# Three one-column constants in one buffer: everything allocated behind them moves down by 64 bytes

## The chip, the core and the metric

The kernel runs on one core of one Trainium2 chip. The metric is the time of one execution on the device, in microseconds (us). Before the change it is 485.12 us, the median of three runs (484.73 to 485.75). Every other number here is of one profiled execution, which itself took 485.06 us, or of the program as it is built (buffer addresses).

## What is computed

The reference is one transformer-like block on a sequence of 2048 rows of 448 channels: a layer norm scaled and shifted by a condition vector, a long convolution over the sequence (a state space model, S4), a gated residual, a second layer norm, and a SwiGLU feed-forward of inner width 1792 with a second gated residual.

```python
def _B_ref(x, w_gate, w_up, w_down):
    g = _silu(x @ w_gate)
    u = x @ w_up
    return (g * u) @ w_down
...
mod = (_silu(c) @ w_mod).reshape(c.shape[0], 6, 1, -1)
sa, ca, ga, sb, cb, gb = (mod[:, 0], mod[:, 1], mod[:, 2], mod[:, 3], mod[:, 4], mod[:, 5])
h = _layernorm(x, axis=-1) * (1 + ca) + sa
x = x + ga * _A_ref(h, A_A_re, A_A_im, A_B_re, A_B_im, A_C_re, A_C_im, A_log_dt, A_Dskip)
h = _layernorm(x, axis=-1) * (1 + cb) + sb
x = x + gb * _B_ref(h, B_w_gate, B_w_up, B_w_down)
return x
```

`_A_ref` is the convolution. On the inputs given its kernel is so close to a straight line over the sequence that the program takes a short way (`small_path`); a flag computed on the chip chooses between it and a general convolution, which does not run here.

## The kernel before, in words

**The head** (0 to about 40 us). Twenty-eight transfers on the SyncE queue bring the six state arrays, the modulation weights (`wm0` to `wm4`, and a sixth group into `m5`), the first rows of `x` and the first feed-forward weights. From these, all engines make the modulation rows, the two slopes of the convolution and the first two row tiles of the second norm. The order is written out by hand in `ORDER` (the loads) and `PLAN` (the compute steps).

**The feed-forward** (about 33 us to the end). The 2048 rows are 16 tiles of 128, worked on in six blocks of 2, 2, 3, 3, 3 and 3 tiles (`BLOCKS`). `ffn` runs for each block over the 14 slices `f` of the inner width. For every `f`, `gate_up` makes two products of 128 by 256 or 128 by 384 in PSUM: 22 matmuls, line 729, all issued by `mm`. The weight slice `wgu[f]` (tile `gu`, 128 by 128 a piece) is the stationary operand and the transposed activations `hhi` and `hlo` are the moving one. Full-precision numbers are split in two parts that the fast float32r format holds, hence eleven matmuls for a product of four pieces. ScalarE applies SiLU (line 744), VectorE multiplies by the up product (line 757), ScalarE and VectorE split the result into `phi` and `plo` (lines 760, 761). `down` then adds to the output in PSUM, three matmuls for each row tile (line 773): `phi` or `plo` stationary, the down weights `wdh` or `wdl` moving, 448 columns. Between these matmuls, VectorE, ScalarE and GpSimd prepare the rows of the next block (`small_path`, `Norm`, `turn`), three TensorE products with the triangular matrix `tri` among it (lines 933 to 935, and 945 to 948 in the first block).

**All weights stay in SBUF.** In the first block the slices are loaded into staging buffers (`raw`, `rawd`) and split into `gu`, `wdh` and `wdl` (lines 112 to 127); the later five blocks load no weights.

**How SBUF is laid out.** Pools hand out addresses along each of the 128 partitions in the order in which tiles are created, each rounded up to 32 bytes. The pool `const` comes first: `x` rows, `m5`, staging, `ident`, `tri`, `run`, `hhi`, `hlo` and others. At its end stand the small constants that the change touches: `ones` (1.0, line 227), `mhalf` (-0.5, line 228), `ntok` (minus the row number, line 229), each of one column of float32, that is 4 bytes a partition in a slot of 32. Behind them lie `cs`, `pick`, `gac`, the small norm tiles, `gu0` to `gu2` with their down weights, then the buffers of the head (`pre`), and over these later `gu3` to `gu13`, the other down weights and the working tiles (`v1`, `vh`, `vl`, `p`, `phi`, `plo`).

`ones` is read by two one-element activations (lines 295, 320), by a copy (line 304) and as a stationary column (line 438); `mhalf` is the exponent of the power in `Norm.root` (line 168, on GpSimd); `ntok` is used once (line 703).

Of the kernel before, what the change touches and what calls it, by code (L numbers as in the profile page):

```python
# [8 lines left out]
F32 = mybir.dt.float32  # L9
# [47 lines left out]
def tile_kernel(ctx, tc, x, a_re, a_im, b_re, b_im, c_re, c_im, log_dt,  # L57
# [5 lines left out]
    const = ctx.enter_context(tc.tile_pool(name="const", bufs=1))  # L63
# [160 lines left out]
            parts(hi, lo, turned[:, 0:m, :, k, :], k)  # L224

    wp0 = ctx.enter_context(tc.tile_pool(name="wp0", bufs=1))
    ones = const.tile([128, 1], F32)
    mhalf = const.tile([128, 1], F32)
    ntok = const.tile([128, 1], F32)
    cs = const.tile([128, 5], F32)  # L230
    pick = const.tile([128, 1], F32)
    gac = const.tile([128, 4], F32)
# [813 lines left out]
def build(nc, aps, out):  # L1046
    with tile.TileContext(nc) as tc:
        a = dict(aps)
        tile_kernel(tc, a["A_u"].rearrange("b l d -> (b l) d"), *[a[n] for n in _INS[1:] + ["B_w_gate_up", "A_states", "w_mod_groups", "c_log_dt", "dft", "idft"]],
                    out.rearrange("b l d -> (b l) d"))  # L1050
# [20 lines left out]
```

## Time and profile before

| | |
|---|---|
| median of three runs | 485.12 us (484.73 to 485.75) |
| the profiled execution's own time | 485.06 us |
| its span, first to last instruction | 483.0 us |
| outside the span | 2.06 us |
| TensorE matmul busy, share of the span | 471.6 us, 98% |
| TensorE weight load busy | 444.9 us, 92% |
| VectorE / ScalarE / GpSimd busy | 285.1 / 155.4 / 59.8 us |
| mean granted TensorE clock | 0.999 |

The span lies between the first and the last instruction that the profiler records. A busy engine is one with an instruction in flight; matmuls overlap each other in the array, so the duration of one (start to end) is longer than the distance from one to the next, and it is the distance that adds up. PE is TensorE's matmul stream, PEld its weight loads, DVE is VectorE, ACT ScalarE, POOL GpSimd, SP SyncE.

### The profile page before, as it was taken

The numbers are of one execution on the slowest core, as the hardware profiler recorded it, in microseconds if no ns is written. First come the engines' busy times: TensorE is split into PE (matmuls) and PEld (weight loads), VectorE is DVE, ScalarE is ACT, GpSimd is POOL, SyncE is SP. The second block draws the span as 40 slices with busy tenths as digits, with TensorE's granted clock in tenths as the row PEclk, the third lists the DMA queues.
The fourth block names the chain that finished last, engine by engine and source line by source line (L and its number), as shares of the span: only waits on it lengthen the run. The fifth ranks groups of instructions, "written<-read, shape, count | busy, mean of one in ns | idle before, by whom it ended". The sixth has DMA issues, their size and how long they took to land.

```text
span 483.0 us, 7024 instructions
## 1 busy us (share of the span) xinstructions
PE 471.6 (98%) x2743; PEld 444.9 (92%) x2743; DVE 285.1 (59%) x550; ACT 155.4 (32%) x336; POOL 59.8 (12%) x82
## 2 busy tenths in 40 slices
PE   6999999999999999999999999999999999999995
PEld 4668988999999999999999999999999999999995
DVE  4879998768876546573644757375475544221225
ACT  5876545522234222332312323331222232112111
POOL 1220000000000040310022221002241000000000
PEclk9999999999999999999999999999999999999999
DMA  8965563020001200111200011130001112000001
GB/s 307 405 225 165 194 188 103 0 96 2 1 2 39 58 1 0 45 38 51 92 25 0 2 44 46 43 115 0 2 2 44 45 43 77 22 1 0 1 1 62
DMA packets 18778, 31.24 MB, mean 65 GB/s; under 512 B 2608, under 2 KB 13488, under 8 KB 18736
## 3 DMA queue, kind: packets, MB, share of 16 engines
q1 hardware_dynamic: 18000, 30.52, 18.8%
q8 instruction: 23, 0.38, 0.3%
q10 hardware_dynamic: 736, 0.19, 0.2%
q14 instruction: 19, 0.16, 0.1%
HBM read 24.61 MB, written 6.03 MB: 63 GB/s over the span
## 4 chain that ended last, share of the span: by engine, by line
PE 92%; DMA 3%; DVE 2%; ACT 1%; issue 0%; POOL 0%; SPq 0%; ACTq 0%; DVEq 0%
PE bank L729 59%; PE dn L773 28%; DMA wm<-in_w_mod_groups_dram 2%; DMA x<-in_A_u_dram 1%; PE bank L238 1%; PE dn L449 1%; PE bank L934 1%; PE cv L933 1%; PE cv L935 0%; PE bank L947 0%; DVE x L812 0%; PE bank L206 0%; PE cv L946 0%; PE cv L948 0%; ACT raw L195 0%
## 5 line engine op out<-in xcount | busy, mean ns | idle before, releaser
L729 PE MATMUL bank<-hhi,gu 128*128 128x384 f32 (+1 forms) x1169 | 211.3, 320 | 0.0
L729 PEld LDWEIGHTS bank<-hhi,gu 128*128 128x128 f32 x1169 | 191.2, 188 | 3.1 <-issue 0.7
L729 PE MATMUL bank<-hlo,gu 128*128 128x384 f32 (+1 forms) x668 | 131.8, 319 | 0.0
L757 DVE TENSOR_TENSOR bank<-raw,bank 128x384 f32<-128x384 f32 (+1 forms) x69 | 36.9, 534 | 125.0 <-PE bank L729 121.6
L729 PEld LDWEIGHTS bank<-hlo,gu 128*128 128x128 f32 x668 | 110.2, 188 | 0.0
L760 ACT CAST phi<-bank 128x384 fp32r<-128x384 f32 (+1 forms) x83 | 36.9, 444 | 141.6 <-DVE bank L757 141.6
L744 ACT ACTIVATE raw<-bank 128x384 f32<-128x384 f32 (+1 forms) x70 | 32.9, 470 | 123.0 <-PE bank L729 114.9
L761 DVE TENSOR_TENSOR plo<-bank,phi 128x384 fp32r<-128x384 f32 (+1 forms) x83 | 42.5, 512 | 37.1 <-ACT phi L760 37.1
L773 PE MATMUL dn<-wdh,phi 128*128 128x448 f32 x218 | 58.3, 368 | 0.6 <-DVE run L698 0.4
L773 PE MATMUL dn<-wdh,plo 128*128 128x448 f32 x218 | 57.7, 366 | 0.0
L773 PE MATMUL dn<-wdl,phi 128*128 128x448 f32 x218 | 57.6, 365 | 0.0
L773 PEld LDWEIGHTS dn<-wdl,phi 128*128 128x128 f32 x218 | 41.0, 188 | 3.4
L773 PEld LDWEIGHTS dn<-wdh,plo 128*128 128x128 f32 x218 | 40.9, 188 | 3.3
L773 PEld LDWEIGHTS dn<-wdh,phi 128*128 128x128 f32 x218 | 38.9, 188 | 2.9 <-DVE run L698 0.7
L167 POOL TENSOR_SCALAR rsb<-mvb 128x1 f32<-128x1 f32 (+2 forms) x13 | 4.6, 354 | 171.9 <-DVE mvb L151 171.9
L167 POOL TENSOR_SCALAR rsa<-mva 128x3 f32<-128x3 f32 (+1 forms) x6 | 2.4, 396 | 116.1 <-DVE mva L151 116.1
L123 ACT CAST gu<-raw 128x1024 fp32r<-128x1024 f32 x14 | 14.6, 1046 | 0.0
L125 DVE TENSOR_TENSOR gu<-raw,gu 128x768 fp32r<-128x768 f32 x14 | 13.3, 953 | 0.1
L922 DVE TENSOR_TENSOR vl<-m,vh 128x448 fp32r<-128x448 f32 x12 | 9.1, 757 | 6.7 <-ACT vh L921 6.1
L908 POOL TENSOR_TENSOR m<-m,gm 128x448 f32<-128x448 f32 x9 | 10.4, 1154 | 21.4 <-DVE m L184 17.5
L194 ACT ACTIVATE raw<-raw,rsb 128x64 f32<-128x64 f32 x14 | 4.8, 346 | 21.0 <-DVE raw L193 11.9
L927 POOL TENSOR_TENSOR m<-m,gd 128x448 f32<-128x448 f32 x9 | 11.6, 1284 | 0.0
(232 smaller groups left out, 411.0 us busy)
## 6 DMA issues: line engine op xcount, KB each, us to landing
raw<-in_B_w_gate_up_dram SPq DMA_DIRECT2D x14, 512.0 KB, 3.9
rawd<-in_B_w_down_dram SPq DMA_DIRECT2D x16, 224.0 KB, 4.1
x<-in_A_u_dram SPq DMA_DIRECT2D x12, 224.0 KB, 3.3
out_dram<-x SPq DMA_DIRECT2D x11, 224.0 KB, 2.0
xd<-raw SPq DMA_DIRECT2D x9, 256.0 KB, 2.0
raw<-xd SPq DMA_DIRECT2D x36, 64.0 KB, 2.0
wm<-in_w_mod_groups_dram SPq DMA_DIRECT2D x5, 448.0 KB, 8.2
wm<-in_w_mod_groups_dram SPq DMA_DIRECT2D x5, 336.0 KB, 8.2
```

The lines of the kernel that those rows point to most:

```text
L123: sc.copy(wgu[j][:, :, 0:4, :], w)
L125: en.tensor_tensor(lo, w[:, :, 0:3, :], f32(hi), op=OP.subtract)
L167: po.tensor_scalar(rs[:, 0:n], self.mv[:, 0:n, 1], EPS, None, op0=OP.add)
L729: pe.matmul(ps[s][:, 0:n], w[:, s, a], (hlo if lo else hhi)[:, k, 0:n], start=first and q == 0, stop=end and q == len(ka) - 1)
L744: sc.activation(p[:, 0:n], ps[0][:, 0:n], AF.Silu)
L757: ve.tensor_tensor(ps[1][:, 0:n], p[:, 0:n], ps[1][:, 0:n], op=OP.mult)
L760: sc.copy(hi[:, 0:n], ps[1][:, 0:n])
L761: ve.tensor_tensor(lo[:, 0:n], ps[1][:, 0:n], f32(hi[:, 0:n]), op=OP.subtract)
L773: pe.matmul(dn[q][:, 0:D], u[:, cs], v, start=f == 0 and z == 0, stop=f == (NF - 3 if last else NF - 1) and z == 2)
L908: (ve if on_v else po).tensor_tensor(v, h, g, op=OP.mult)
L922: ve.tensor_tensor(vl, v0, f32(vh), op=OP.subtract)
L927: (ve if on_v else po).tensor_tensor(h, h, gd, op=OP.mult)
```

## The change

The three constants become the three columns of one tile. The names stay and refer to its columns.

```diff
     wp0 = ctx.enter_context(tc.tile_pool(name="wp0", bufs=1))
-    ones = const.tile([128, 1], F32)
-    mhalf = const.tile([128, 1], F32)
-    ntok = const.tile([128, 1], F32)
+    few = const.tile([128, 3], F32)
+    ones, mhalf, ntok = (few[:, q:q + 1] for q in range(3))
     cs = const.tile([128, 5], F32)
     pick = const.tile([128, 1], F32)
     gac = const.tile([128, 4], F32)
```

Three slots of 32 bytes become one, so that what is allocated behind them lies 64 bytes lower on each partition. In the built programs:

| buffer | address before | after | rest by 128 before | after |
|---|---|---|---|---|
| `x`, `m5`, `raw`, `rawd`, `ident`, `tri` | 1152 to 37248 | the same | 0 | 0 |
| `run`, `hhi`, `hlo` | 37792 to 54688 | the same | 32 | 32 |
| `ones`, `mhalf`, `ntok` | 62688, 62720, 62752 | 62688, 62692, 62696 | 96, 0, 32 | 96, 100, 104 |
| `cs` | 62784 | 62720 | 64 | 0 |
| `gu0` to `gu13` | 63264 to 195872 | 64 lower | 32 | 96 |
| `wdh`, `wdl`, `v1`, `vh`, `vl`, `p`, `phi`, `plo` | 77600 and up | 64 lower | 32 | 96 |
| `wm0` to `wm4`, the states, `h`, `v0`, `v1` of the head | 95584 and up | 64 lower | 96 | 32 |
| `ramp`, `far`, `all1` of the head | 148992 and up | 64 lower | 0 | 64 |

No instruction is added, removed or moved on any engine, and each waits for the same semaphores and values as before; only the names and the addresses differ, and the line numbers, by one. GpSimd's first compute rows show it. Before (`J`, `tok` and `ntok` are filled, then the first norm's power is taken):

```order
L289 IOTA J 128x128
L290 IOTA tok 128x1
L291 IOTA ntok 128x1
L167 TENSOR_SCALAR rsa<-mva 128x2
L168 TENSOR_TENSOR rsa<-rsa,mhalf 128x2
```

After, on the same engine and at the same place:

```order
L288 IOTA J 128x128
L289 IOTA tok 128x1
L290 IOTA few 128x1
L167 TENSOR_SCALAR rsa<-mva 128x2
L168 TENSOR_TENSOR rsa<-rsa,few 128x2
```

Nothing moved: the third fill and the power name `few` in place of `ntok` and `mhalf`.

## The prediction

> **What bounds the kernel now.** I read the busy times first, then the shares of the chain that ended last, then the waits, then the chain in order of time.
>
> The page, parts 1 and 4:
>
> ```profile
> PE 471.6 (98%) x2743; PEld 444.9 (92%) x2743; DVE 285.1 (59%) x550; ACT 155.4 (32%) x336; POOL 59.8 (12%) x82
> ...
> PE 92%; DMA 3%; DVE 2%; ACT 1%; issue 0%; POOL 0%; SPq 0%; ACTq 0%; DVEq 0%
> ```
>
> TensorE is busy 98% of the span and makes 92% of the chain that sets the end. The waits say the same from the other side (engine and line, what it waited for, us in total, times, longest):
>
> ```profile
> DVE bank L757 <- PE bank L729: 121.6, 57, 4.0
> ACT raw L744 <- PE bank L729: 114.9, 54, 3.2
> ```
>
> VectorE and ScalarE wait for gate and up matmuls, not the reverse. Split at 40 us (length, then busy time of each engine; PEclk is the granted clock):
>
> ```profile
> core 0: us, PE busy (x) PEld busy (x) DVE busy (x) ACT busy (x) POOL busy (x), PEclk, DMA share, GB/s
> 0.00:40.00 40.00, 34.13 (x192) 22.62 (x192) 29.51 (x73) 27.83 (x69) 8.85 (x21) 1.00 0.80 293
> 40.00:483.00 443.00, 437.44 (x2551) 422.23 (x2551) 255.56 (x478) 127.61 (x267) 50.97 (x61) 1.00 0.14 44
> ```
>
> There are two regimes: 40 us of head, in which transfers and every engine take turns, and 443 us in which TensorE is idle for 5.6 us only, at full clock. So the time is the head plus a matmul count times the distance between matmuls. Those distances are in the chain in order of time (start us, length us, what):
>
> ```profile
> 24.37 0.75 PE dn L481 x2
> ...
> 56.75 2.61 PE bank L729 x22
> ...
> 64.63 0.75 PE cv L946 x2
> ...
> 198.01 3.86 PE bank L729 x22
> ...
> 464.53 3.88 PE bank L729 x22
> 468.41 1.82 PE dn L773 x9
> 470.23 3.89 PE bank L729 x22
> ```
>
> A burst of 22 gate and up matmuls takes 2.61 us with 256 moving columns (118.6 ns each) and 3.86 to 3.89 with 384 (175.5 to 176.8 ns); a down matmul with 448 columns takes 1.82 / 9 = 202 ns. There are 2 x 14 = 28 short bursts (616 matmuls), 4 x 14 = 56 long ones (1232), and 16 tiles x 14 x 3 = 672 down matmuls: 73 + 217 + 136 = 426 us of the 443. **Only what changes the distance of these matmuls can move the time much.** One ns on each of the 1848 gate and up matmuls is 1.85 us, or 0.4%.
>
> **The change, part by part.**
>
> *Instructions and waits.* None is added, removed or moved, and no wait has another semaphore or value. Had the shared buffer tied its readers to all three writers, this would show what it costs (tile, times in ns, first and last start):
>
> ```profile
> L291 POOL IOTA ntok<- x1: 131/131/131, 1.1 to 1.1; 128x1 f32 x1
> L292 DVE MEMSET ones<- x1: 59/59/59, 0.8 to 0.8; 128x1 f32 x1
> L304 DVE CAST all<-ones x1: 220/220/220, 1.6 to 1.6; 128x128 fp32r<-128x128 f32 x1
> ```
>
> The last writer ends at 1.1 + 0.13 = 1.23 us and the first reader starts at 1.6. Such a wait would be over before it began: 0 us either way.
>
> *The head.* The states, `wm0` to `wm4` and the working tiles go from rest 96 by 128 to rest 32. Buffers at other rests do the same work in this trace. Transfers of 448 KB (KB, us to landing) into `wm` (rest 96) and `m` (the tile `m5`, rest 0):
>
> ```profile
> wm<-in_w_mod_groups_dram SPq DMA_DIRECT2D x5, 448.0 KB, 8.2
> m<-in_w_mod_groups_dram SPq DMA_DIRECT2D x1, 448.0 KB, 8.3
> ```
>
> One VectorE operation, writing `m` (rest 0) and `h` of the head (rest 96), min/median/max ns:
>
> ```profile
> L182 DVE SCALAR_TENSOR_TENSOR m<-rawd,mva,ca x4: 677/677/680, 105.6 to 255.5; 128x448 f32<-128x448 f32 x4
> L182 DVE SCALAR_TENSOR_TENSOR h<-x,mva,ca x2: 680/680/681, 15.1 to 15.7; 128x448 f32<-128x448 f32 x2
> ```
>
> They differ by 0.1 us and by 3 ns, and the order in the queue alone would explain as much. The full float32 matmuls above move `v0` of the head at rest 96 (line 481) and `m5` at rest 0 (line 946): 0.75 us for two in both. I take 0 for the head, between -0.1 and +0.1 us.
>
> *The down matmuls.* Their stationary `phi` and `plo` and their moving `wdh` and `wdl` all move together, so that their distance in memory stays. By operand (busy us, mean ns):
>
> ```profile
> L773 PE MATMUL dn<-wdh,phi 128*128 128x448 f32 x218 | 58.3, 368 | 0.6 <-DVE run L698 0.4 <-ACT x L697 0.2
> L773 PE MATMUL dn<-wdl,phi 128*128 128x448 f32 x218 | 57.6, 365 | 0.0
> ```
>
> `wdl` lies 1792 bytes behind `wdh`, that is, half of 512 off, and nothing but the waits ahead of the first of each group tells them apart. I take 0.
>
> *The gate and up matmuls.* Here is the one relation that changes: moving `hhi` and `hlo` stay at rest 32, stationary `gu` goes from rest 32 to 96. Every weight load runs beside the matmul before it, so two reads of SBUF that used to be equal by 128 are now 64 bytes apart. No row has just this pair. Nearest are float32r matmuls of 448 columns with other pairs:
>
> ```profile
> L934 PE MATMUL bank<-v,tri 128*128 128x448 f32 x12 | 4.4, 366 | 0.0
> L933 PE MATMUL cv<-vh,tri 128*128 128x448 f32 x12 | 4.4, 365 | 0.0
> ...
> L449 PE MATMUL dn<-v,far 128*128 128x448 f32 x1 | 0.4, 369 | 0.0
> ```
>
> `tri` is at rest 0 beside moving `v1` and `vh` at 32 (a difference of 32): 366 and 365 ns. `far` is at 0 beside the head's `v1` at 96: 369, a single one. Against 365 to 368 of line 773, where both are at 32, no row shows a relation that costs or saves more than a few ns. **I take 0**, the value of these rows.
>
> The ends come from the pace. A full float32 matmul of 448 columns takes 0.75 / 2 = 375 ns. If that is two passes, one pass of 448 is 187.5 ns, of 384 160.7 and of 256 107.1. The bursts need 175.9 (3.87 us) and 118.6: 15.2 and 11.5 ns more, on which no view puts a name. If the shift took all of it away, it would save 15.2 x 1232 + 11.5 x 616 = 25.8 us: **459.3** is the low end. For the high end, each matmul is as long as the longest (min/median/max, then means by shape):
>
> ```profile
> L729 PE MATMUL bank<-hhi,gu x1169: 274/336/384, 33.7 to 473.1; 128*128 128x384 f32 x130, 128*128 128x256 f32 x65
> L729 PE MATMUL bank<-hlo,gu x668: 277/336/343, 35.7 to 473.8; 128*128 128x384 f32 x112, 128*128 128x256 f32 x55
> L729 PE MATMUL dn<-hlo,gu x4: 279/280/285, 35.3 to 35.6; 128*128 128x256 f32 x4
> ```
>
> ```profile
> L729 PE MATMUL bank<-hlo,gu 128*128 128x384 f32 x448 | 96.8, 338 | 0.0
> ...
> L729 PE MATMUL bank<-hlo,gu 128*128 128x256 f32 x220 | 34.9, 282 | 0.0
> ```
>
> With 343 for 338 and 285 for 282: 5 x 1232 + 3 x 616 = 8.0 us, or **493.1**.
>
> *A rule beside it.* The Trainium skill, page "TensorE: Matmul & The Clock Gate", section "Step-by-step: what each phase is for", says that TensorE reads the moving operand and the weights through two independent ports, so that loading the next weights takes nothing from the running matmul; by that rule the new distance between `gu` and `hhi` cannot matter and the sum stays at 485.1. The trace agrees in the three pairs of rests above (32 and 32, 0 and 32, 0 and 96). The same page, section "Back-to-back issue gap", gives N / 2.4 + 2.5 ns for a warm matmul: 162.5 ns at 384 columns and 109.2 at 256. The trace shows 175.9 and 118.6, so this rule does not describe this stream, and by it a shift that freed the stream would end at an estimated 485.1 - 13.4 x 1.232 - 9.4 x 0.616 = 462.8.
>
> **The sum.** 485.06 (own time of the profiled execution: 483.0 of span and 2.06 around it) + 0 + 0 + 0 = 485.06. That execution lies 0.06 under the median of the runs, 485.12. I predict 485.1.
>
> **The rivals.**
>
> *Faster: the long step goes.* The durations at 384 columns are not one value: most are at 336, some at 343, with a mean of 338. Equal work with two lengths says that something beats against the stream. If it is the weight load beside it, a new distance can take the step away: 338 to 336 on 1232 matmuls and 282 to 280 on 616 gives 2.5 + 1.2 = 3.7 us: **481.4**. For it: 15 ns above the pace on every matmul, unexplained. Against it: bursts with quite different neighbours on VectorE and the other engines agree within 3.86 to 3.89, and three pairs of rests show nothing. Any larger gain, down to 459.3, is its tail.
>
> *Slower: the step comes more often.* The same mechanism at the same place, with the other sign: the weight load of matmul n + 1 now meets the moving read of matmul n in the same part of SBUF. If the long step comes twice as often, the means rise by 2 ns: +3.7 us, **488.8**; with every step long 493.1. It decides from about half a ns a matmul on (0.97 us / 1848). For it: both reads used to be in the same phase by 128 and that phase may be the good one. Against it: `far` beside `v1` is out of phase and 369 ns long, as the slowest of line 773.
>
> *The change does not do what it says.* Rounding could have kept the addresses. It didn't: `gu0` goes from 63264 to 63200. No chance.
>
> **How the numbers follow.** No change 0.45, faster 0.32, slower 0.23. The rows speak for no change, but none has the pair at stake, and 1848 matmuls turn one ns into 0.4%, so that I don't go higher. Faster gets more than slower since its room is wider (25.8 us against 8.0). A measurement of this kernel can tell about 0.2% (1 us) from no change; the likeliest case alone has the range 484.1 to 486.1. The whole range takes in both rivals' prices and some of their tails, 480.5 to 489.0; left out are about 0.11 below and 0.09 above.
>
> **What would show it.** Right: bursts of line 729 again 2.61 and 3.86 to 3.89 us, means 338 and 282, line 773 at 365 to 368, and from 40 us on 5 to 6 us of idle TensorE. Faster or slower by address: these means shift on line 729 and not on line 773, in all six blocks alike. If line 773 shifts too, my claim that only the distance between operands counts is wrong, and the place of one operand alone matters. If the first 40 us take longer and the bursts don't, the head's addresses matter. What would make the prediction wrong is a change of half a ns or more in the distance of the gate and up matmuls.

## The result, and the profile after

The changed kernel takes **483.22 us** (median of six runs, 482.81 to 484.40) against 485.09 us for the kernel before (six runs): a ratio of 0.9963, with a 95% interval of 0.9951 to 0.9976. It is faster by 0.37%, or 1.9 us. I had forecast no change. The profiled execution took 484.40 us, the longest of the six.

Everything in the program is the same but addresses, so the profile has to be read for durations alone. The page, parts 1 and 4:

```profile
PE 471.0 (98%) x2743; PEld 443.4 (92%) x2743; DVE 285.2 (59%) x550; ACT 155.4 (32%) x336; POOL 59.9 (12%) x82
...
PE 92%; DMA 3%; DVE 2%; ACT 1%; issue 0%; SPq 0%; POOL 0%; POOLq 0%; ACTq 0%; DVEq 0%
```

The bound has not moved, and no other engine does more or less work. The two stages, split at 40 us as before:

```profile
0.00:40.00 40.00, 34.91 (x192) 23.26 (x192) 29.11 (x73) 27.82 (x69) 8.97 (x21) 1.00 0.79 290
40.00:482.40 442.40, 436.06 (x2552) 420.14 (x2551) 256.05 (x478) 127.61 (x267) 50.91 (x61) 1.00 0.14 44
```

From 40 us on it is 442.40 us instead of 443.00, at the same granted clock, and TensorE is still idle for some 6 us of it. So the same matmuls went through TensorE in less time. The chain in order of time shows which (start us, length us, what; the line numbers are one lower than before):

```profile
1.64 5.25 DMA x<-in_A_u_dram
...
57.18 2.59 PE bank L728 x22
...
101.74 2.51 PE bank L728 x22
...
458.13 3.89 PE bank L728 x22
462.02 1.82 PE dn L772 x9
463.84 3.84 PE bank L728 x22
467.68 1.84 PE dn L772 x9
469.53 3.90 PE bank L728 x22
```

The short bursts of gate and up matmuls took 2.61 us and take 2.59 in the first block and mostly 2.51 in the second. The long ones took 3.86 to 3.89 us and are now mostly 3.84 or 3.89, which take turns here. The groups of nine down matmuls, 1.82 before at this place, alternate between 1.82 and 1.84. The first transfer on the chain, of `x`, whose buffer did not move, was shorter before:

```profile
1.64 4.56 DMA x<-in_A_u_dram
```

In the other runs whose chain begins with it, it took 4.30 to 5.56 us, one execution each, with `x` always at the same address. Behind it, the first down matmul on the chain past 40 us starts 0.5 us later (40.62 for 40.12 us) in this execution. This is a part of why it is the slowest of the six, 1.2 us over their median; the rest is not explained.

The same by shape (busy us, mean ns):

```profile
L728 PE MATMUL bank<-hlo,gu 128*128 128x384 f32 x448 | 96.7, 337 | 0.0
...
L772 PE MATMUL dn<-wdh,phi 128*128 128x448 f32 x218 | 58.4, 368 | 0.7 <-DVE run L697 0.4 <-ACT x L696 0.2
...
L728 PE MATMUL bank<-hlo,gu 128*128 128x256 f32 x220 | 34.3, 279 | 0.0
```

338 became 337, 282 became 279, 368 stayed. These durations hide much, since matmuls overlap. Better is the distance from the start of one matmul to the start of the next, worked out from the starts in the trace, over the pairs under 260 ns (for the down matmuls, without the five shortest, 86 to 117 ns, at the kernel's end): at 256 columns 119.1 before and 116.5 after, at 384 columns 176.0 and 175.6, and for the down matmuls 203.4 and 204.0. On 616, 1232 and 672 matmuls that is -1.6, -0.5 and +0.4 us: **-1.7 us**. The medians differ by 1.9. The profiled executions differ by 0.7 only (484.40 for 485.06), since two things stand against the gain there: the 0.5 us of late start, and a wait that the kernel before does not have. Between the second and the third block TensorE now reaches the transposes (products with `ident`) earlier and waits for ScalarE:

```profile
147.78 0.33 PE L206 MATMUL bank<-ident,raw 128*128 128x128 f32 x1 [0.36 <-ACT raw L195]
```

### The profile page after: what moved, and what is told of

Its sections match the earlier page's. It is cut to its first block, busy times and chain, and to the rows that moved or that the text cites. A ratio compares the mean times of both kernels' runs of the same rounds, so it can differ in the third digit from the quotient of the medians.

```text
span 482.4 us, 7024 instructions
## 1 busy us (share of the span) xinstructions
PE 471.0 (98%) x2743; PEld 443.4 (92%) x2743; DVE 285.2 (59%) x550; ACT 155.4 (32%) x336; POOL 59.9 (12%) x82
## 4 chain that ended last, share of the span: by engine, by line
PE 92%; DMA 3%; DVE 2%; ACT 1%; issue 0%; SPq 0%; POOL 0%; POOLq 0%; ACTq 0%; DVEq 0%
PE bank L728 59%; PE dn L772 28%; DMA wm<-in_w_mod_groups_dram 2%; DMA x<-in_A_u_dram 1%; PE bank L237 1%; PE dn L448 1%; PE bank L933 1%; PE cv L934 1%; PE cv L932 1%; PE bank L946 0%; DVE x L811 0%; PE bank L206 0%; PE cv L947 0%; PE cv L945 0%; ACT raw L195 0%
## 5 line engine op out<-in xcount | busy, mean ns | idle before, releaser
L125 DVE TENSOR_TENSOR gu<-raw,gu 128x768 fp32r<-128x768 f32 x14 | 13.3, 953 | 0.1
```

Source lines behind the costliest of these rows:

```text
L125: en.tensor_tensor(lo, w[:, :, 0:3, :], f32(hi), op=OP.subtract)
```

## The experiments

**The theory** at the start: the pace of the gate and up matmuls depends on the distance in memory between their moving operand (`hhi`, `hlo`) and their stationary one (`gu`). **The rivals**: the weights' own place (rest 96 by 128 is better than 32, whatever `hhi` does), and the shared buffer itself. Every kernel is the one before or the changed one with a few lines edited that move addresses. None leaves work out, and the times of before in each comparison are of the same chip.

### One part alone: the shared buffer without the shift

```diff
-    few = const.tile([128, 3], F32)
-    ones, mhalf, ntok = (few[:, q:q + 1] for q in range(3))
+    few = const.tile([128, 24], F32)
+    ones, mhalf, ntok = (few[:, q:q + 1] for q in (0, 8, 16))
```

> The three constants share one buffer, but it is 96 bytes wide with a constant every 32 bytes, so that every address of the kernel before stays. Theory of the distance (the 64 bytes between the moving hhi/hlo and the stationary gu, by 128, set the pace of the gate and up matmuls): 485.1 us, bursts of 22 on the gate and up line again 2.61 and 3.86 to 3.89 us. Theory of the shared buffer (one tile instead of three by itself): 483.2 us, bursts 2.50 to 2.59 and 3.82 to 3.89. Theory of the weights' own place (rest 96 by 128 is good for gu, whatever hhi is): 485.1.

Measured: 485.28 us against 485.36, ratio 0.9998 (0.9988 to 1.0009). Its chain:

```profile
56.77 2.62 PE bank L728 x22
...
462.78 1.82 PE dn L772 x9
464.60 3.88 PE bank L728 x22
```

The bursts are those of before. The shared buffer is worth nothing that can be measured; the 0.37% is the shift.

### The same distance with the weights in their old place

To the changed kernel, ahead of `hhi`:

```diff
+    padh = const.tile([128, 16], F32)
     hhi = const.tile([128, 4, MB * 128], F32R)
```

> The change plus an unused buffer of 64 bytes ahead of hhi: hhi and hlo go up to rest 96, gu and all that lies behind return to the addresses of before (rest 32). Theory of the distance: 483.2 us and the bursts of the changed kernel, 2.50 to 2.59 and 3.82 to 3.89, since gu and hhi are 64 apart again. Theory of the weights' own place: 485.1 and the bursts of before, 2.61 and 3.87. The down matmuls as before in both, 1.82 to 1.83 us for nine.

Measured: 483.25 us against 485.36, ratio 0.9958 (0.9944 to 0.9973). The chain:

```profile
59.88 2.51 PE bank L729 x22
...
449.03 1.84 PE dn L773 x9
450.88 3.89 PE bank L729 x22
...
456.59 3.84 PE bank L729 x22
```

All weights stand where they stood before, of the operands of these matmuls only `hhi` and `hlo` moved, and the gain is there with the same bursts, 2.51, 3.84 and 3.89. The down matmuls alternate between 1.82 and 1.84 here too, which I had not expected. **The weights' own place is not the cause.**

### The weights in their new place with the old distance

The same line added to the kernel before, so that `hhi` and all behind it go up together.

> The kernel before plus an unused buffer of 64 bytes ahead of hhi: hhi, hlo, gu and everything behind go up by 64 together, gu stands at rest 96 as in the changed kernel, and so does hhi. Theory of the distance: 485.1 us, bursts 2.61 and 3.87. Theory of the weights' own place: 483.2 us, bursts 2.50 to 2.59 and 3.82 to 3.89.

Measured: 485.32 us against 485.36, ratio 0.9996 (0.9986 to 1.0006).

```profile
57.03 2.61 PE bank L730 x22
...
464.79 3.88 PE bank L730 x22
```

`gu` stands at rest 96 by 128, as in the changed kernel, and the buffers of the head stand at their new rests by 128 too; nothing is gained. With the two runs before it, this settles that the distance counts. The head's addresses are worth nothing that can be measured: here they moved and nothing was gained, and in the run before they stayed and the whole gain was there.

### The other distance: the down matmuls

In the kernel before, one working tile is made 64 bytes longer, so that `p`, `phi` and `plo` behind it move and the down weights don't:

```diff
-            vl = work.tile([128, D], F32R, name="vl")
+            vl = work.tile([128, D + 16], F32R, name="vl")[:, 0:D]
```

> The kernel before with one working tile (vl) 64 bytes longer, so that phi and plo, the stationary operands of the down matmuls, go up by 64 and all weights and hhi stay. Theory of the distance, carried to the down matmuls: their pace moves from 1.82 to 1.83 us for nine to something else, up to 2% of their 136 us, so 482.4 to 487.8, and the gate and up bursts keep 2.61 and 3.87 on the mean. If the distance matters for gate and up only: 485.1 and nothing moves.

Measured: 483.87 us against 485.36, ratio 0.9967 (0.9956 to 0.9979). By operand:

```profile
L773 PE MATMUL dn<-wdh,phi 128*128 128x448 f32 x218 | 57.9, 366 | 0.6 <-DVE run L698 0.4 <-ACT x L697 0.2
L773 PE MATMUL dn<-wdh,plo 128*128 128x448 f32 x218 | 57.4, 364 | 0.0
L773 PE MATMUL dn<-wdl,phi 128*128 128x448 f32 x218 | 57.3, 364 | 0.0
```

The distance of the down matmuls falls from 203.4 to 201.9 ns, those of gate and up stay at 119.1 and 175.9. On 672 matmuls that is 1.0 us of the 1.5 that the median fell by. The rule is not one of the gate and up products: each stream has a pace that goes with the distance of its own two operands.

### Both distances together

The changed kernel with the longer `vl`.

> The change and the 64 bytes between phi and the down weights together: gu 64 from hhi, phi and plo 64 from wdh and wdl. Theory of the distance: the two gains add, 2.1 us and 1.5 us, so 481.7 (481.0 to 482.6). If there is one gain only, by some common start phase of the stream: 483.2.

Measured: 481.19 us against 485.22, ratio 0.9914 (0.9902 to 0.9927).

```profile
444.29 3.82 PE bank L728 x22
449.93 3.82 PE bank L728 x22
455.57 3.82 PE bank L728 x22
```

The gains add, and the half microsecond more is at the edge of what these intervals can tell. The bursts are clearer: the long ones take 3.82 us, with few exceptions, where the changed kernel has 3.84 and 3.89 with the very same `hhi` and `gu`; the down matmuls (202.5 ns) have no such extra. So the distance of a stream's own two operands does not fix its pace alone. It looks as if a stream can run in more than one repeating pattern, and as if the stream ahead of it, at the handover, decides which. The distance from `hhi` to `phi` across the handover changed as well, and no run separates the two.

### Other distances: 32, 96 and 128 bytes up

The kernel before with an unused buffer of 32, 96 or 128 bytes behind `gac`, which moves the weights and all behind them:

```diff
     gac = const.tile([128, 4], F32)
+    padw = const.tile([128, 8], F32)
```

> The kernel before with 32 unused bytes ahead of the weights: gu (and all behind) at rest 64, hhi at 32, a distance of 32. Theory of the distance by lines of 64 bytes: a half step decides nothing new, so one of the two values seen, 485.1 or 483.2. Theory that any 32 bytes count: a third value, bursts outside of both 2.61/3.87 and 2.50 to 2.59/3.82 to 3.89. Down bursts as before, 1.82, since phi and wdh move together.

> The kernel before with 96 unused bytes ahead of the weights: gu at rest 0, hhi at 32, the distance 32 the other way. Same two theories as with 32 bytes; if lines of 64 bytes decide, this one gets the other value than 32 bytes up or the same.

> The kernel before with 128 unused bytes ahead of the weights: all rests by 128 as before, only the distance by 256 changes. If the distance counts by 128: 485.1 and bursts 2.61 and 3.87. If it counts by 256 or more: another time, within 483 to 487, with other bursts.

Measured: 32 up gives 486.41 us, ratio 1.0035 (1.0020 to 1.0050), **slower**; 96 up 484.24, ratio 0.9984 (0.9975 to 0.9994); 128 up 484.31, ratio 0.9979 (0.9968 to 0.9989), all against 485.22. The chains, in this order:

```profile
56.73 2.64 PE bank L730 x22
...
465.85 3.88 PE bank L730 x22
```

```profile
56.83 2.57 PE bank L730 x22
...
457.96 3.89 PE bank L730 x22
461.85 1.83 PE dn L774 x9
463.68 3.81 PE bank L730 x22
467.49 1.86 PE dn L774 x9
```

```profile
57.68 2.64 PE bank L730 x22
...
458.69 3.82 PE bank L730 x22
462.50 1.85 PE dn L774 x9
464.36 3.82 PE bank L730 x22
```

Two versions of my theory fall. It is not lines of 64 bytes, since 32 and 96 give values of their own. And it is not the distance by 128, since 128 bytes up make the short bursts longer (2.64), the long ones shorter (3.82) and the down matmuls slower (1.85), although these keep their own distance, which fits the handover.

### The distance by 256

> The kernel before with four small constants (ones, mhalf, ntok, cs) allocated ahead of hhi: hhi and hlo go up by 128, all weights and working tiles stay. The distance between hhi and gu is then, by 256, that of the run with the weights 128 up. Theory of the distance, now by 256: 484.3 us as there, gate and up bursts 2.63 to 2.64 and 3.82, down 1.85. Theory that the weights' place by 256 counted there: 485.1 and bursts 2.61 and 3.87.

> The kernel before with the row tile gd (1792 bytes, 7 times 256) allocated ahead of hhi: hhi and hlo go up by 1792, all else stays. By 256 every distance is as before, by 512 it is 256 off. If the distance counts by 256: 485.1, bursts 2.61 and 3.86 to 3.88. If it counts by 512 or more: another time, 481 to 487, with other bursts.

> The kernel before with 64 unused bytes ahead of the weights: they go up by 64 where the change takes them down by 64. By 128 gu stands at the same rest 96 as in the changed kernel, by 256 it does not. If the distance counts by 128: 483.2, bursts 2.50 to 2.59 and 3.82 to 3.89. If by 256, as the run with 128 bytes says: another time (481 to 487) and other bursts.

The first takes four small constants, the second the row tile `gd`, from behind `hhi` to ahead of it; the third is `padw` with 64 bytes. Measured: `hhi` up by 128, 483.76 us against 485.24, ratio 0.9974 (0.9961 to 0.9986); up by 1792, 485.20, ratio 1.0000 (0.9988 to 1.0011); weights up by 64, **481.64**, ratio 0.9925 (0.9911 to 0.9940). The chains, in this order:

```profile
57.48 2.64 PE bank L729 x22
...
462.23 1.85 PE dn L773 x9
464.08 3.82 PE bank L729 x22
```

```profile
56.70 2.61 PE bank L729 x22
...
464.53 3.88 PE bank L729 x22
468.41 1.82 PE dn L773 x9
```

```profile
455.05 3.81 PE bank L730 x22
458.87 1.82 PE dn L774 x9
460.69 3.81 PE bank L730 x22
464.50 1.82 PE dn L774 x9
```

`hhi` up by 128 agrees with the run with the weights up by 128, with other buffers moved: the same bursts, and distances from start to start within 0.3 ns. `hhi` up by 1792, which is 7 times 256, is the kernel before. **The distance counts by 256 bytes.** And 64 up is not 64 down: the same rest by 128, but twice the gain.

This also says why one shift reaches the whole stream. The slices of `gu` are 7168 bytes long (28 times 256) with down weights of twice 1792 between them (14 times 256), and the four parts of `hhi` are 1536 apart (6 times 256): every one of the 1848 matmuls has the same distance by 256, and one small constant ahead of the weights shifts them all.

### The best distances together

From the runs so far I set both distances to 64 by 256: the six small constants go ahead of `hhi` (up by 192), and `vl` is 192 bytes longer.

```diff
+    ones = const.tile([128, 1], F32)
+    mhalf = const.tile([128, 1], F32)
+    ntok = const.tile([128, 1], F32)
+    cs = const.tile([128, 5], F32)
+    pick = const.tile([128, 1], F32)
+    gac = const.tile([128, 4], F32)
     hhi = const.tile([128, 4, MB * 128], F32R)
...
-            vl = work.tile([128, D], F32R, name="vl")
+            vl = work.tile([128, D + 48], F32R, name="vl")[:, 0:D]
```

> All six small constants allocated ahead of hhi (hhi and hlo go up by 192, the weights stay) and vl 192 bytes longer (phi and plo go up by 192). By 256 hhi is then 64 above gu, as in the run with the weights 64 up, and wdh and wdl are 64 above phi and plo, a distance not tried for the down matmuls. Theory of the distance by 256: gate and up bursts 2.59 and 3.82 as in that run, so 481.6 or less; the down matmuls move from 202.6 ns to another pace; if 64 is as good for them as for gate and up (two quanta of 6.67 ns above 28), 200 ns and 479.9 us. If the weights' place counts instead: 485.1.

Measured: **479.56 us** against 485.42, ratio 0.9890 (0.9874 to 0.9905), 1.1% faster than the kernel before and faster than the changed one. The chain, and the durations of the gate and up matmuls (min/median/max ns):

```profile
56.79 2.59 PE bank L729 x22
59.39 1.21 PE dn L773 x6
...
457.67 1.80 PE dn L773 x9
459.47 3.81 PE bank L729 x22
463.29 1.80 PE dn L773 x9
```

```profile
L729 PE MATMUL bank<-hlo,gu x668: 276/336/336, 35.9 to 468.6; 128*128 128x384 f32 x112, 128*128 128x256 f32 x55
```

The long step is gone: the longest of 668 matmuls is now the median, 336 ns, where the kernel before had 343. The down matmuls take 1.80 / 9 = 200 ns, as the expectation had it for the case that 64 suits them as well. (Its 6.67 ns are 16 columns at 2.4 columns a ns, so that 448 columns are 28 such units; no run shows that a pace has to be a whole number of them.)

### All runs by distance

Distances are `hhi` minus `gu` and `wdh` minus `phi`, by 256, from the addresses; ns are the mean distances from start to start, as above.

| kernel | `hhi` - `gu` | `wdh` - `phi` | 256 columns, ns | 384 columns, ns | down, ns | ratio |
|---|---|---|---|---|---|---|
| before | 128 | 0 | 119.1 | 176.0 | 203.4 | 1 |
| shared buffer, no shift | 128 | 0 | 119.1 | 176.0 | 203.5 | 0.9998 |
| all up 64 | 128 | 0 | 119.0 | 176.2 | 202.9 | 0.9996 |
| `hhi` up 1792 | 128 | 0 | 119.1 | 176.0 | 203.5 | 1.0000 |
| **the change** | 192 | 0 | 116.5 | 175.6 | 204.0 | 0.9963 |
| `hhi` up 64, weights in place | 192 | 0 | 115.3 | 175.7 | 203.9 | 0.9958 |
| weights up 32 | 96 | 0 | 120.3 | 176.5 | 203.8 | 1.0035 |
| weights up 96 | 32 | 0 | 117.1 | 175.5 | 204.1 | 0.9984 |
| weights up 128 | 0 | 0 | 120.1 | 173.6 | 205.4 | 0.9979 |
| `hhi` up 128 | 0 | 0 | 120.1 | 173.8 | 205.1 | 0.9974 |
| weights up 64 | 64 | 0 | 118.1 | 173.4 | 202.6 | 0.9925 |
| `phi` up 64 | 128 | 192 | 119.1 | 175.9 | 201.9 | 0.9967 |
| the change and `phi` up 64 | 192 | 192 | 116.4 | 173.6 | 202.5 | 0.9914 |
| both distances 64 | 64 | 64 | 118.2 | 173.4 | 200.5 | 0.9890 |

Kernels with the same two distances agree in their times, wherever the buffers stand. Kernels with other distances differ in their paces, though not always in their times: the intervals of 32 and of 0 overlap (0.9984 and 0.9979), since at 0 the long bursts are shorter than at 32, and the short ones and the down matmuls longer.

## Why the prediction was right or wrong

The measured 483.22 us lies inside the whole range, 480.5 to 489.0, and below the range of the likeliest case, 484.1 to 486.1. The whole range held because it was made wide enough for the rivals; the case that it was built around, with a chance of 0.45, did not come, and "faster", with 0.32, did.

**The forecast of no change failed at one step: "I take 0, the value of these rows", for the gate and up matmuls.** Measured instead: -2.6 ns at 256 columns and -0.4 at 384, -2.1 us together. What I named as a rival, a shorter distance between these matmuls, is what happened.

- *What bounds the kernel* held: the gain is in the distance of these matmuls. Against it stood 0.4 us at the down matmuls, and in the profiled execution the 0.5 us of late start and 0.4 us of new wait for ScalarE, for which the sum had no term.
- *Instructions, waits and the shared buffer* at 0 held: 0.9998.
- *The head* at 0 held: with its buffers at their new rests and the old distance, the ratio is 0.9996. The 0.5 us that the profiled execution lost there came behind the transfer of `x`, whose buffer did not move.
- *The down matmuls* at 0 were right in the reason, that their own distance stays, and off by 0.4 us: their pace moved although their own distance did not, as that of the stream ahead of them moved. I had written that a shift on line 773 would mean that the place of one operand counts. It shifted, and the run with the weights in their old place shows that this reading was wrong: 203.9 ns there, with `phi` and `wdh` where they were before.
- *The gate and up matmuls.* Each of the three rows on which I took 0 was weak, and could have been seen to be. I sorted operands by their rest by 128, and 256 is what counts: `wdl` lies 1792 bytes behind `wdh`, which is 7 times 256, so that the two rows that I compared have the same distance and could not differ. The matmuls with `tri` and `far` come in threes or alone. In a pattern that repeats only after several matmuls, such rows may show the handover and not the pace. And a mean duration rounded to a ns, of matmuls that overlap, was the wrong ruler where half a ns decides.
- *The rival "the long step goes"* had the place, and half of what happens there. Its price, 3.7 us or 481.4, was twice what the change brought. The step did go: of the 1232 matmuls at 384 columns, 290 took 340 ns or more before and 3 do in the changed kernel. But the others got longer: 100 took 338 or 339 ns before, and 811 do now. The stream runs in another pattern, and not in the old one without its step. With the weights up by 64, 1181 of them take 336 or 337 ns. There the price came near: the distances fall by 2.6 ns at 384 columns and 1.0 at 256, which is 3.2 + 0.6 = 3.8 us on 1232 and 616, where I had 2.5 + 1.2, and the time fell by 3.6.
- *The rival "the step comes more often"* exists too, at another distance: weights up by 32, +0.35%.
- *The rule beside it.* The Trainium skill, page "TensorE: Matmul & The Clock Gate", section "Step-by-step: what each phase is for", has the weight load and the moving operand on independent ports, so that loading the next weights takes nothing from the running matmul. By it, the distance between the two could not matter; here the distances of the two streams move the time by up to 1.1% with nothing but addresses changed, and the measurement decides. The page's gap of N / 2.4 + 2.5 ns for a matmul by itself (section "Back-to-back issue gap"), 162.5 ns at 384 columns, was reached at no distance tried: the best is 173.4.

What is shown is that the distance by 256 bytes between a matmul's moving and stationary operands goes with its pace, and that moving one against the other changes it. That `gu` is the partner of `hhi`, and not the down weights that lie between its slices, follows from the operands of these matmuls; no run moved the two apart. That the handover from the stream ahead plays a part is inferred from paces that moved at an unchanged distance. That it is the load of the next weights that meets the moving read in SBUF is argued from this and not shown. No run took the load away. What decides between two patterns at the same distances stays open as well: the changed kernel's short bursts take 2.59 us in the first block and 2.51 in most of the second, at unchanged addresses.

## What to carry to other kernels

Where a float32r matmul stream bounds a kernel, as here, the addresses of its two operands can be a tuning parameter like any other: step the one against the other by 32 or 64 bytes over 256 and measure, in both directions, since here the range is from +0.35% to -1.1%. Keep slice lengths at multiples of 256, so that one step moves the whole stream, and recheck after any edit that allocates a small buffer ahead of the weights, since that alone can move the time by some tenths of a per cent and be taken for an effect of the edit. To see such an effect in a profile, take the length of whole bursts from the chain in order of time, not mean durations.

## What the runs showed of the hardware that I had not expected

- The bursts crowd at a few lengths: 3.81 to 3.82, 3.84, 3.86 to 3.88 and 3.89 us for 22 matmuls of 384 columns, and 2.51, 2.57, 2.59, 2.61 and 2.64 at 256. Different kernels return to the same ones; besides, each kernel has one longer burst, of 2.71 to 2.83 us. It looks like a stream that locks into one of a few repeating patterns.
- The best paces are 173.4 ns at 384 columns (3.81 to 3.82 us / 22) and 200.0 at 448 (1.80 us / 9). The 64 columns between them cost 26.6 ns, 2.4 columns a ns, and at that rate both leave 13.3 ns a matmul over, as two points on a line must. The best at 256 columns, 115.3 ns, leaves less: 8.6.
- Full float32 matmuls of 448 columns take 375 ns for each of two, both with `v0` beside `all1` (a distance of 96 by 256) and with `m5` beside `tri` (0). No run changed either distance, so whether such a stream would show the effect stays open.
- A stream's pace can depend on more than its own two operands: at the same `hhi` and `gu`, long bursts took 3.84 and 3.89 us, or 3.82 nearly all, as only `p`, `phi` and `plo` moved by 64 bytes.
